# Loads of the opening in another order, one bias row, a later weight conversion and a second buffer for the thresholded low part, in a spectral layer with a gated feed-forward

## The chip, the core and the metric

One NeuronCore of one Trainium2 chip runs the whole program. The time is the device's, in microseconds, for one execution. Engines: TensorE (PE, with its weight loads PEld), VectorE (DVE), ScalarE (ACT), GpSimd (POOL), and SyncE (SP), whose queue issues every DMA of this kernel. Every engine takes its instructions in order.

## What is computed

Eight sequences of 3136 rows of 256 floats go through a spectral layer and a gated feed-forward layer:

```python
X = rfft(x, axis=1)                      # x: 8 x 3136 x 256
Yr = Xr @ w_r - Xi @ w_i + b_r           # w: 256 x 256
Yi = Xr @ w_i + Xi @ w_r + b_i
Y = softshrink(Yr, 0.01) + 1j * softshrink(Yi, 0.01)
x = irfft(Y, n=3136, axis=1)
h = relu(x @ w_in)                       # w_in: 256 x 1024
c = conv3_along_rows(h, conv_w)          # depthwise, 3 taps
out = (h * sigmoid(c)) @ w_out           # w_out: 1024 x 256
```

w_in, conv_w and w_out come as 64-bit floats.

## The kernel before

**Stages.** The transform of 3136 = 56 x 56 points is done in two factors. Stage 1 multiplies x by f1 (seven column groups per batch, `stage1`, for batch 0 `stage1_head`) and stores the result to DRAM (sc1). From there the work runs in 56 steps (batch b, frequency group g of seven): `load_a2` reads a group of sc1 back across the batch (so the first of a batch needs all seven stores of that batch), `stage2` multiplies by t2 and splits the result into a high and a low part (fh, fl), `mix` multiplies by the weights W with three products each, adds the bias and thresholds to v, and splits v into sh (ACT) and sl (GpSimd, line 321), and `stage3` multiplies by inv1 and stores to DRAM (sc2). Then stage 4 and the feed-forward layer (`up`, `down`) run from sc2.

**The loop.** Iteration `it` loads a2 of step it+2, runs stage 2 of step it, mix of step it-1, stage 3 of step it-3 and one or two further groups of stage 1 of a later batch. In its first seven iterations it also loads inv1 of group it (to be split by ACT and DVE, lines 140 and 141) and t2 of group it+1.

**The background.** `later` converts the 64-bit conv_w (cw), w_in and w_out on DVE and ACT, as a generator that is advanced a few pieces in each iteration: 3 x 7 pieces for cw, then nine for each of eight weight tiles, of which one only asks for bits. The bits have two buffers.

**What sets the order.** A planner places the instructions of each engine by the order of the program and by when their inputs are ready in its own forecast, and puts in all waits. `tc.issue_after(ins)` queues what its block traces on the engine of `ins` behind `ins`, on that engine alone: around loads that means SP's queue, around the threshold (line 319) DVE's. SP holds a DMA back until its data may be touched, and all that stands behind it waits too. Buffers: a2 has three, raw (for W and inv1) two, sh two, sl one.

**Lines of the steps below.** 140 and 141 split inv1; 147 loads t2; 153 W; 163 the bias; 168 inv1; 236 x; 245 and 246 stage 1 and its copy by ACT; 265 stores batch 0's stage 1; 270 loads a2; 280 stage 2; 283 to 288 its splitting; 304 mix; 309 adds the bias; 313 combines to v; 319 thresholds; 320 and 321 split v; 331 stage 3.

Of the kernel before, what the change touches and what calls it, by code (L numbers as in the profile page):

```python
# [9 lines left out]
F32 = mybir.dt.float32  # L10
F32R = mybir.dt.float32r
# [3 lines left out]
ALU = mybir.AluOpType  # L15
# [10 lines left out]
UG = 4  # L26
NG = U // UG
# [69 lines left out]
def spectral_ffn_kernel(ctx: ExitStack, tc: tile.TileContext, x, w_r, w_i, b_r, b_i,  # L97
# [19 lines left out]
    with ExitStack() as ab:  # L117
# [14 lines left out]
        cmx.tile([P, 96], F32, name="pad")  # L132
        bias = cmx.tile([P, 2, UG // 2, D], F32, name="bias")
        wmix_hi = cmx.tile([P, NT, 3, D], F32R, name="wmix_hi")
# [11 lines left out]
        def load_t2(g):  # L146
            nc.sync.dma_start(t2[:, g * UG:(g + 1) * UG, :], fwd2v[:, g * UG:(g + 1) * UG, :])
# [12 lines left out]
        def load_bias():  # L160
            for c in range(2):
                for k in range(UG // 2):
                    nc.sync.dma_start(bias[:, c, k, :], (b_r, b_i)[c].partition_broadcast(P))

# [42 lines left out]
        def later():  # L207
# [13 lines left out]
            asked = []  # L221
            for n in range(len(pieces) + 1):
                if n < len(pieces):
                    dst, src, nm = pieces[n]
                    asked.append((dst, load_bits(src, WP, nm), WP, nm))
                    yield None
                if n:
                    yield from split_weight(*asked.pop(0))

# [61 lines left out]
        def mix(xs):  # L291
# [16 lines left out]
            for c in range(2):  # L308
                nc.vector.tensor_tensor(p1[:, c], ps[2], bias[:, c], op=ALU.add)
            for c in range(2):  # L310
# [4 lines left out]
            sh = wk.tile([K2, UG, D], F32R, name="sh")  # L315
            sl = wk.tile([K2, UG, D], F32R, name="sl", bufs=1)
            r = wk.tile([K2, UG, D], F32, name="r", bufs=1)
# [24 lines left out]
        n_it = len(items)  # L342
        WP0, CW_IT = 3, 9
        a2s = {}
        p1 = NG
        load_f1()
        with tc.tile_pool(name="hx", bufs=1, reuse_waits="tile") as hx:
            xh = []
            for p in range(NG):
                xr, ld = load_x(hx, 0, p, parts=2 if p == 0 else 1, tag=f"hx{p}")  # L350
                xh.append(xr)
            with tc.issue_after(ld.ins):
                load_t2(0)
                load_mix()
                load_bias()
                st = stage1_head(xh)
        with tc.issue_after(st.ins):
            for _ in range(2):
                stage1(*items[p1])
                p1 += 1  # L360
            for i in range(2):
                a2s[i], ld = load_a2(*items[i])
        ab.enter_context(tc.issue_after(ld.ins))
# [9 lines left out]
        for it in range(n_it + 3):  # L373
            if it + 2 < n_it:
                a2s[it + 2], _ = load_a2(*items[it + 2])
            if it < n_it:
                xs[it] = stage2(items[it][1], a2s.pop(it))
            if it < NG:
                load_inv1(it)
                if it + 1 < NG:  # L380
                    load_t2(it + 1)
            if 0 <= it - 1 < n_it:
                ss[it - 1] = mix(xs.pop(it - 1))
            if 0 <= it - 3 < n_it:
                stage3(*items[it - 3], ss.pop(it - 3))
            while p1 < n_it and p1 < min(it + AHEAD, NG + 2 + it + it // 2):
                stage1(*items[p1])
                p1 += 1
            if WP0 <= it < n_it:
                with tc.issue_after(ss[it - 1][2].ins):  # L390
                    for _ in range(5 if it < CW_IT else 2 + (it % 5 == 0)):
                        next(background, None)
# [148 lines left out]
```

## Time and profile before

| | us |
|---|---|
| median of three runs | 1771.51 (1766.52 to 1772.43) |
| the profiled execution | 1769.05 |
| its span, first to last instruction | 1767.3 |
| PE busy | 1731.0 (98% of the span) |
| DVE busy | 1524.3 (86%) |
| ACT busy | 1229.1 (70%) |
| GpSimd busy | 134.7 (8%) |

The profile is one execution. Busy time says how long an engine had an instruction under way; the idle time before an instruction is put down to what released it last. Matmuls are pipelined, so PE's busy time counts overlapping instructions once. A DMA's landing is when its data are in place.

### The profile page before, as it was taken

The page shows a single profiled execution, that of the slowest core. Times are in us where ns is not written, and L with a number is a line of the kernel's source. Part 1 is how long each engine was busy: PE and PEld are TensorE (multiplying, and loading weights), DVE is VectorE, ACT ScalarE, POOL GpSimd, SP SyncE. Part 2 cuts the span into 40 slices and gives each one's busy share as a digit, 9 for nine tenths or more (in the row PEclk, how much of TensorE's full clock was granted, in tenths as well). Part 3 has the DMA queues.
Part 4 walks back from the last instruction along what each step waited for, and adds up shares of the span by engine and source line. Part 5 has one row for each costly group of instructions (what it writes and reads, how often), then busy time and mean ns, then how long its engine had stood idle before and what let it go on. Part 6 is the DMA issues. An engine that isn't in the chain of part 4 may idle for free.

```text
span 1767.3 us, 29387 instructions
## 1 busy us (share of the span) xinstructions
PE 1731.0 (98%) x12096; PEld 1621.6 (92%) x12096; DVE 1524.3 (86%) x1820; ACT 1229.1 (70%) x1590; POOL 134.7 (8%) x60
## 2 busy tenths in 40 slices
PE   6899999999998999999999999999999999999999
PEld 2788888888998999999999999999999999999998
DVE  2899999998896988988888888888888888888887
ACT  2667777776665777777777777777777777777766
POOL 0122222222232000000000000000000000000000
PEclk8999999999999999999999999999999999999999
DMA  9777677677534110111111011111101111100001
GB/s 263 216 230 236 196 232 216 192 230 228 164 111 136 43 43 22 32 53 53 32 53 53 22 55 51 49 46 52 43 22 43 53 43 43 42 22 22 22 22 42
DMA packets 107382, 164.63 MB, mean 93 GB/s; under 512 B 8816, under 2 KB 86000, under 8 KB 107248
## 3 DMA queue, kind: packets, MB, share of 16 engines
q1 hardware_dynamic: 107248, 162.74, 30.9%
q8 instruction: 96, 1.57, 0.4%
q14 instruction: 38, 0.31, 0.1%
HBM read 85.65 MB, written 77.07 MB: 92 GB/s over the span
## 4 chain that ended last, share of the span: by engine, by line
PE 93%; DMA 3%; DVE 1%; ACT 1%; issue 0%; SPq 0%; ACTq 0%
PE acc L470 31%; PE ps_h L442 31%; PE ps_mx L304 12%; PE ps_s L423 5%; PE ps_s L280 5%; PE ps_s L331 4%; PE ps_s L245 4%; DMA i_raw<-in_inv_dram 2%; DMA z<-sc 1%; DMA sc<-ha 0%; DMA a<-sc 0%; DMA sc<-a 0%; ACT a L246 0%; DVE cw L212 0%; DVE yl L430 0%
## 5 line engine op out<-in xcount | busy, mean ns | idle before, releaser
L470 PE MATMUL acc<-wout,gh 128*128 128x256 f32 x3136 | 567.0, 280 | 0.0
L451 DVE SCALAR_TENSOR_TENSOR c<-h,cw,c 128x896 f32<-128x896 f32 x448 | 513.1, 1147 | 47.3 <-ACT c L449 46.3
L442 PE MATMUL ps_h<-yh,win 128*128 128x450 f32 x1792 | 551.0, 368 | 0.1
L470 PEld LDWEIGHTS acc<-wout,gh 128*128 128x128 f32 x3136 | 493.7, 188 | 6.5
L470 PE MATMUL acc<-wout,gl 128*128 128x256 f32 x1568 | 437.6, 281 | 0.0
L444 ACT ACTIVATE h<-ps_h 128x900 f32<-128x900 f32 x224 | 207.7, 927 | 254.8 <-PE ps_h L442 254.8
L442 PEld LDWEIGHTS ps_h<-yh,win 128*128 128x128 f32 x1792 | 338.7, 189 | 26.4 <-DVE yl L430 0.8
L442 PE MATMUL ps_h<-yl,win 128*128 128x450 f32 x896 | 329.2, 367 | 0.0
L470 PEld LDWEIGHTS acc<-wout,gl 128*128 128x128 f32 x1568 | 293.7, 188 | 0.1
L457 DVE TENSOR_TENSOR gl<-c,gh 128x896 fp32r<-128x896 f32 x224 | 243.1, 1089 | 53.6 <-ACT gh L456 50.1
L453 DVE TENSOR_TENSOR c<-h,c 128x896 f32<-128x896 f32 x224 | 243.6, 1088 | 46.9 <-ACT c L452 46.7
L456 ACT CAST gh<-c 128x896 fp32r<-128x896 f32 x224 | 209.8, 942 | 49.4 <-DVE c L453 49.4
L452 ACT ACTIVATE c<-c 128x896 f32<-128x896 f32 x224 | 213.3, 952 | 23.9 <-DVE c L451 21.0
L304 PE MATMUL ps_mx<-wmix_lo,fh 128*128 128x256 f32 x672 | 202.2, 301 | 0.0
L304 PE MATMUL ps_mx<-wmix_hi,fh 128*128 128x256 f32 x672 | 196.9, 294 | 0.5 <-DVE v L313 0.3
L304 PE MATMUL ps_mx<-wmix_hi,fl 128*128 128x256 f32 x672 | 188.7, 282 | 1.3 <-DVE fl L288 1.2
L442 PEld LDWEIGHTS ps_h<-yl,win 128*128 128x128 f32 x896 | 168.9, 189 | 11.0
L449 ACT ACTIVATE c<-h,cw 128x896 f32<-128x896 f32 x168 | 175.5, 1044 | 2.6 <-DVE gl L457 0.2
L321 POOL TENSOR_TENSOR sl<-v,sh 128x1024 fp32r<-128x1024 f32 x56 | 134.5, 2402 | 423.1 <-PE ps_s L331 300.0
L313 DVE TENSOR_TENSOR v<-ps_mx,p 64x512 f32<-64x512 f32 x224 | 154.0, 688 | 3.3
L304 PEld LDWEIGHTS ps_mx<-wmix_lo,fh 128*128 128x128 f32 x672 | 126.4, 188 | 12.3 <-issue 12.3
L304 PEld LDWEIGHTS ps_mx<-wmix_hi,fl 128*128 128x128 f32 x672 | 126.0, 188 | 11.8 <-issue 9.9
(84 smaller groups left out, 2023.0 us busy)
## 6 DMA issues: line engine op xcount, KB each, us to landing
a<-sc SPq DMA_DIRECT2D x56, 448.0 KB, 5.0
sc<-z SPq DMA_DIRECT2D x56, 448.0 KB, 3.3
z<-sc SPq DMA_DIRECT2D x56, 448.0 KB, 3.8
xr<-in_x_dram SPq DMA_DIRECT2D x55, 448.0 KB, 4.7
out_dram<-o SPq DMA_DIRECT2D x27, 896.0 KB, 4.0
sc<-a SPq DMA_DIRECT2D x49, 448.0 KB, 4.9
sc<-ha SPq DMA_DIRECT2D x7, 448.0 KB, 7.5
win_bits<-in_moe_w_in_dram SPq DMA_DIRECT2D x4, 512.0 KB, 7.6
```

Source lines behind the costliest of these rows:

```text
L304: nc.tensor.matmul(ps[c][:, k, :], lt, rh, start=(n == 0), stop=(n == len(mm) - 1))
L313: nc.vector.tensor_tensor(v[dst, :, k, :], ps[c][src], p1[src, c], op=ALU.add)
L321: SL_ENG.tensor_tensor(sl, v, sh.bitcast(F32), op=ALU.subtract)
L442: nc.tensor.matmul(ps[:, a, 0:CH + 2], lt, rh, start=(n == 0), stop=(n == len(mm) - 1))
L444: nc.scalar.activation(h, ps[:, :, 0:CH + 2], AF.Relu)
L449: nc.scalar.mul(c, h[:, :, 0:CH], cw[:, 0, f:f + 1])
L451: nc.vector.scalar_tensor_tensor(c, h[:, :, k:k + CH], cw[:, k, f:f + 1], c, op0=ALU.mult, op1=ALU.add)
L452: nc.scalar.activation(c, c, AF.Sigmoid)
L453: nc.vector.tensor_tensor(c, h[:, :, 1:CH + 1], c, op=ALU.mult)
L456: nc.scalar.copy(gh, c)
L457: nc.vector.tensor_tensor(gl, c, gh.bitcast(F32), op=ALU.subtract)
L470: nc.tensor.matmul(acc[m // 2][:, m % 2, :], lt[:, sl], rh[:, f, :], start=(f == 0 and n == 0 and m % 2 == 0), stop=(f == NF - 1 and n == ...
```

## The change

Bias goes from two copies per part to one (two DMAs in place of four), and line 309 reads it with a broadcast over the two halves. In the opening, W is loaded ahead of t2 of group 0; the first a2 load comes right behind batch 0's last store, the bias and the second a2 behind it, and the two stage-1 groups of batch 1 come after them. In the first five iterations t2 of the next group and inv1 of this one are queued on SP behind the a2 load of this iteration, t2 first. The conversion starts in iteration 7 in place of 3, with two and three pieces in turn in place of five (up to iteration 8) and then two or, every fifth time, three. The bits of a weight tile are asked for after five pieces of the one before. sl gets two buffers.

```diff
-        bias = cmx.tile([P, 2, UG // 2, D], F32, name="bias")
+        bias = cmx.tile([P, 2, D], F32, name="bias")
...
             for c in range(2):
-                for k in range(UG // 2):
-                    nc.sync.dma_start(bias[:, c, k, :], (b_r, b_i)[c].partition_broadcast(P))
+                nc.sync.dma_start(bias[:, c, :], (b_r, b_i)[c].partition_broadcast(P))
...
             for n in range(len(pieces) + 1):
+                work = split_weight(*asked.pop(0)) if n else iter(())
+                for _ in range(5):
+                    if n:
+                        yield next(work)
                 if n < len(pieces):
                     dst, src, nm = pieces[n]
                     asked.append((dst, load_bits(src, WP, nm), WP, nm))
                     yield None
-                if n:
-                    yield from split_weight(*asked.pop(0))
+                yield from work
...
-                nc.vector.tensor_tensor(p1[:, c], ps[2], bias[:, c], op=ALU.add)
+                nc.vector.tensor_tensor(p1[:, c], ps[2], bias[:, c].unsqueeze(1).broadcast_to([K2, UG // 2, D]), op=ALU.add)
...
-            sl = wk.tile([K2, UG, D], F32R, name="sl", bufs=1)
+            sl = wk.tile([K2, UG, D], F32R, name="sl", bufs=2)
...
-        WP0, CW_IT = 3, 9
+        WP0 = NG
...
             with tc.issue_after(ld.ins):
+                load_mix()
                 load_t2(0)
-                load_mix()
-                load_bias()
                 st = stage1_head(xh)
         with tc.issue_after(st.ins):
+            a2s[0], ld = load_a2(*items[0])
+        with tc.issue_after(ld.ins):
+            load_bias()
+            a2s[1], ld = load_a2(*items[1])
             for _ in range(2):
                 stage1(*items[p1])
                 p1 += 1
-            for i in range(2):
-                a2s[i], ld = load_a2(*items[i])
         ab.enter_context(tc.issue_after(ld.ins))
...
             if it + 2 < n_it:
-                a2s[it + 2], _ = load_a2(*items[it + 2])
+                a2s[it + 2], ld = load_a2(*items[it + 2])
...
             if it < NG:
-                load_inv1(it)
-                if it + 1 < NG:
-                    load_t2(it + 1)
+                with tc.issue_after(ld.ins) if it + 2 < NG else ExitStack():
+                    if it + 1 < NG:
+                        load_t2(it + 1)
+                    load_inv1(it)
...
                 with tc.issue_after(ss[it - 1][2].ins):
-                    for _ in range(5 if it < CW_IT else 2 + (it % 5 == 0)):
+                    for _ in range(2 + it % 2):
                         next(background, None)
```

## Rows read from the trace of the kernel before

**Rows 1.** The page's first part: busy us (share), instructions.

```profile
PE 1731.0 (98%) x12096; PEld 1621.6 (92%) x12096; DVE 1524.3 (86%) x1820; ACT 1229.1 (70%) x1590; POOL 134.7 (8%) x60
```

**Rows 2.** Busy time by stretch: length, engines busy (instructions), PE clock, DMA share, GB/s.

```profile
23.00:32.60 9.60, 0.00 (x0) 0.01 (x1) 1.18 (x2) 0.34 (x1) 0.00 (x0) 0.71 0.95 317
32.60:42.00 9.40, 7.77 (x25) 5.24 (x26) 1.53 (x3) 2.55 (x6) 0.00 (x0) 0.57 1.10 244
42.00:75.00 33.00, 28.01 (x197) 23.77 (x198) 27.11 (x45) 18.81 (x35) 2.41 (x1) 1.00 0.92 242
75.00:125.00 50.00, 47.51 (x342) 41.09 (x340) 45.74 (x83) 33.91 (x59) 13.75 (x6) 1.00 0.72 210
125.00:390.00 265.00, 265.00 (x1969) 235.76 (x1969) 251.68 (x409) 191.86 (x305) 69.10 (x30) 1.00 0.73 217
390.00:480.00 90.00, 90.00 (x676) 80.59 (x675) 77.79 (x123) 59.93 (x99) 22.88 (x11) 1.00 0.66 195
```

**Rows 3.** PE's waits, whole span: us in total, times, longest.

```profile
PE ps_s L245 <- ACT a L246: 6.0, 5, 2.2
```

**Rows 4.** ACT's waits from 40 to 130 us: total, times, longest.

```profile
ACT i_hi L140 <- DMA i_raw<-in_inv_dram: 12.4, 6, 4.3
```

**Rows 5.** The chain that ended last: start us, us, what.

```profile
24.25 6.40 DMA sc<-ha
...
99.89 3.08 DMA sc<-a
...
102.98 4.20 DMA a<-sc
...
125.69 0.86 PE ps_s L245 x2
126.55 3.39 PE ps_mx L304 x29
```

**Rows 6.** Timeline of PE: start, us, instruction, shape, count [idle before, releaser].

```profile
35.97 3.79 PE L280 MATMUL ps_s<-t,a 112*128 112x128 f32 x16 [1.33 <-DMA a<-sc]
...
41.86 1.13 PE L280 MATMUL ps_s<-t,a 112*128 112x128 f32 x8 [0.28 <-DMA t<-in_fwd_dram]
```

**Rows 7.** Line 163, loads of the bias: durations ns, first and last start, landing.

```profile
L163 SPq DMA_DIRECT2D bias<-in_b_r_dram x2: 346/346/346, 10.1 to 11.7; - x2
L163 SPq DMA_DIRECT2D bias<-in_b_i_dram x2: 328/328/328, 13.4 to 14.8; - x2
...
DMA to landing us min/median/max: 8.0/8.6/9.1
```

**Rows 8.** Line 236 from 24 to 27 us, x of batch 1.

```profile
L236 SPq DMA_DIRECT2D xr<-in_x_dram x2: 893/952/1012, 24.6 to 25.5; - x2
...
DMA to landing us min/median/max: 7.9/8.2/8.4
```

**Rows 9.** Timelines of DVE, ACT and GpSimd within one steady step.

```profile
255.11 1.23 DVE L319 SCALAR_TENSOR_TENSOR v<-v,r 128x1024 f32<-128x1024 f32 x1
...
259.05 0.69 DVE L288 TENSOR_TENSOR fl<-d,fh 128x512 fp32r<-128x512 f32 x1
...
263.19 0.42 DVE L285 TENSOR_TENSOR d<-ps_s,d 128x256 f32<-128x256 f32 x1 [0.74 <-ACT fh L284]
...
264.24 1.23 DVE L319 SCALAR_TENSOR_TENSOR v<-v,r 128x1024 f32<-128x1024 f32 x1
...
256.57 1.06 ACT L320 CAST sh<-v 128x1024 fp32r<-128x1024 f32 x1
...
260.56 2.36 POOL L321 TENSOR_TENSOR sl<-v,sh 128x1024 fp32r<-128x1024 f32 x1 [6.76 <-PE ps_s L331]
```

**Rows 10.** Groups of DVE instructions by line, 400 to 480 us: busy, mean ns, idle.

```profile
L309 DVE TENSOR_TENSOR p<-ps_mx,bias 128x512 f32<-128x512 f32 x18 | 11.5, 682 | 0.0
```

**Rows 11.** GpSimd's timeline at 81 us; durations of line 188 on cw (min/median/max ns).

```profile
81.43 2.36 POOL L321 TENSOR_TENSOR sl<-v,sh 128x1024 fp32r<-128x1024 f32 x1 [3.75 <-PE ps_s L331]
...
L188 DVE SCALAR_TENSOR_TENSOR cw_e<-cw_bits,cw_e x3: 161/167/1744, 82.1 to 110.4; 128x8 int32<-128x8 int32 x3
```

## Prediction, made before the changed kernel ran

> **What bounds the kernel now.** I read the engines' busy times first: TensorE (PE) is busy in 1731.0 of 1767.3 us [rows 1]. So a change that only reorders loads and moves side work can return at most the 36 us in which PE is not busy, and of those only what lies in the part it touches. The stage windows say where they are [rows 2]. From 125 to 390 us, the steady run of loop steps, PE is busy in 265.00 of 265.00 us: nothing is to be had there, only to be lost. The opening holds the rest: PE does nothing from 23.0 to 32.6 us (9.6 us), is busy in 7.77 of 9.40 us up to 42 us at a mean granted clock of 0.57 (partly at the lower of its two levels, after the idle stretch), and then leaves 33.00 - 28.01 = 5.0 us (42 to 75) and 50.00 - 47.51 = 2.5 us (75 to 125). Who ends the later waits: ScalarE's (ACT) copy of the stage-1 result, 6.0 us in 5 waits [rows 3], and ACT itself stands 12.4 us for the loads of inv1, which sit in its in-order queue [rows 4].
>
> **How the opening is chained.** The chain of waits says: the last store of batch 0's stage 1 leaves at 24.25 and lands 6.40 us later, at 30.65 [rows 5]; the first load_a2 reads all seven stores back, and PE's first stage-2 matmul starts at 35.97, released by that load [rows 6]. The loads land one behind the other. The first bias copy lands at 10.1 + 9.1 = 19.2, the last at 14.8 + 8.0 = 22.8 (1.2 us each), the two stage-1 loads of batch 1 at 24.6 + 7.9 = 32.5 and 25.5 + 8.4 = 33.9, and a2(0) at 35.9, 2.0 us after them [rows 6 to 9].
>
> **The change, part by part.**
>
> *Bias loaded once, behind the first a2; stage-1 loads behind it too.* Four bias DMAs ahead of the stores (3.6 us of the DMA queue from the first landing to the last) become two behind a2(0); two 448 KB loads (1.4 us each in the queue) go behind a2(1). With the bias gone the stores could land at 30.65 - 3.6 = 27.0. But the last store's issue at 24.25 also waits for its copy, and a store with an empty queue takes 3.08 us (99.89 to 102.97, same size) [rows 5]: 27.3 is the later of the two. A lone a2 load took 4.20 us (102.98 to 107.18) [rows 5], so a2(0) lands at 27.3 + 4.2 = 31.5 where it was 35.9: **4.4 us earlier**. What is late next is t2(1), which the second step needs. By the new order it stands behind two bias copies (2.4 us at the old rate), a2(1) (2.0), two xr (2.8) and a2(2) (2.0), and takes about 1.0 itself, half of an a2: 31.5 + 10.2 = 41.7, against 41.86 before, when PE's second step started on exactly this load [rows 6]. So the second step does not move; the gain stays only if PE fills 31.5 to 41.7 with work: stage 2 of step 0 (3.79 us at the low clock [rows 6]), mix of step 0 (36 matmuls at 3.39/29 = 0.117 us [rows 5], 4.2 us), two stage-1 groups (8 records at 0.86/2 us [rows 5], 3.4 us): 11.4 us for 10.2. Before, 25 records had run by 42.0 [rows 2]: stage 2 of step 0, four of stage 1 and the first of mix, 6.0 us of it. Upper bound 4.4 us. Lower bound 0: PE's instructions stand in a fixed order, and if stage 2 of step 1 stands ahead of most of mix(0), as it does now (it came after four of the 36), PE waits for t2(1) as before. I take **3.5**, since mix(0) is ready some 2 us sooner than t2(1) lands.
>
> *t2 and inv1 behind the a2 two steps ahead.* The order becomes that of need; at present inv1 of a step and t2 of the next may overtake the a2 that is wanted sooner. Nothing is removed from the queue. What may go is part of ACT's 12.4 us behind inv1 [rows 4] and with it the 6.0 us of PE behind ACT's copies [rows 3]. inv1 itself lands no earlier, so half may well stay. A new wait comes in: a2(3) to a2(6) wait for stage 2 of the step three before to free a buffer, and t2 and inv1 are queued behind them on SP; they are needed a step or more after that (9 us, below), and a load takes 4.2 us alone and 8.4 behind a queue [rows 5, 8], so I cost it at nothing; without that cover such a step would lose up to 4.2 us.
>
> *Conversion from step 7 instead of 3.* It takes cw's chain out of the DVE queue in the stretch from 75 us, where DVE is busy 45.74 of 50.00 us [rows 2], and i2 and the loads of cw out of SP's queue in the opening. Together with the reorder, the 7.5 us that PE leaves between 42 and 125 us are the upper bound, 0 the lower (the waits behind inv1 stay). I take **4**.
>
> *Conversion at 2.5 pieces a step, later bits.* The steady step is 264.24 - 255.11 = 9.13 us [rows 9]. DVE is busy 251.68/265 of it with the conversion (8.67 us) and 77.79/90 after it (7.89) [rows 2]: 0.78 us for 2.2 pieces, 0.355 each. At 2.5 it is 8.78 us, leaving 0.35 us a step. The 93 pieces (3 x 7 + 8 x 9) last 37 steps, to step 43 of 56; stage 4, which takes over that memory and needs the results, comes 12 steps or 110 us later, so the later end costs nothing. Bits asked for five pieces into the previous weight still have over a step to land: nothing, and at worst one wait of about 8 us on DVE at the first weight.
>
> *Bias as a broadcast operand.* 682 ns for 512 elements from PSUM and SBUF [rows 10]; the strided reads of the other lines cost the same per element, so nothing. At worst each of the two halves pays the 0.42 us of a 256-element instruction (line 285) [rows 9], 0.16 more for each of two instructions, 0.3 a step, which would use up the 0.35.
>
> *Two buffers for sl.* Now GpSimd's subtraction waits for stage 3 of the step before: it starts at 260.56 after standing idle 6.76 us for it, though its input was done at 256.57 + 1.06 = 257.63 [rows 9]. With two buffers it starts there and runs 2.36 us, to 260.1. PE gains nothing: stage 3 comes later anyway and PE is full. But DVE has an instruction with two SBUF inputs there, the low part of d (line 288, at 259.05) [rows 9]. The trace shows what such a meeting costs: GpSimd ran from 81.43 to 83.79, and a tiny DVE instruction with two SBUF inputs that started at 82.1 ended with it, after 1.74 us, where the other two of its line took 0.16 [rows 11]. So line 288 would lose about 0.95 us in a step like this; its place moves with the conversion pieces ahead of it (512 elements each, like its own 0.69 us at most), so with three pieces it falls partly or wholly behind the window. Bounds: 0 and 0.95 us a step, against 0.35 us of slack and an idle 0.74 us ahead of line 285 [rows 9]. I take 0.4 on average, nearly all inside the slack: **1 us late** in all, ends 0 and 37 x 0.60 = 22 us.
>
> The Trainium skill (page "SBUF — State Buffer", section "Who interferes with whom") says that a DVE instruction with two SBUF inputs contends with a GpSimd one that reads SBUF, and that the second to issue blocks until the first ends. The 1.74 us row agrees. Taken at its hardest, a meeting in every step, it gives the third rival below.
>
> **Sum.** 3.5 + 4 - 1 = 6.5 us. The profiled execution took 1769.05 us (span 1767.3); the median of the runs is 1771.51, their mean 1770.15. I take the sum from the middle of these: 1770.2 - 6.5, **1764 us**.
>
> **Rivals.** (1) *Given back at the second step.* PE stands at t2(1) with mix(0) behind it, and ACT at inv1(0), which now lands after t2(1), at about 42. The first term is 0 to 1 and the second 0 to 2: 1769. For: the present order has just this form. Against: ACT's 12.4 us were worst where inv1 ran far behind a full queue, and the queue is shorter now. (2) *All of the opening's later waits go.* 4.4 + 7.5: 1758. For: they hang on one engine's order. Against: the DMA share is 0.92 up to 75 us [rows 2], so part is bandwidth. (3) *Slower: DVE becomes the bound.* If GpSimd's new place costs DVE more than 0.35 us in the mean step, PE falls behind by the difference in each of 37 steps. At 0.7 that is 13 us, so 1777; at the full 0.95, 22 us, 1786; with the opening's gain lost as well, more. For: the step shown; against: the piece order shifts line 288 out of the window as DVE falls late. (4) *It does not do what it says*: the planner orders SP's queue as before; 1770.
>
> **How the numbers follow.** Chances: forecast 0.42 (1760 to 1768), rival 1 0.20, rival 2 0.15, rival 3 0.20 (half of it beyond 1776), rival 4 0.03. About 0.3%, 5.3 us, is what a measurement of this kernel can tell from no change: faster means under 1766.2, slower over 1776.8. Faster: three quarters of the forecast's case and all of rival 2, 0.47. Slower: half of rival 3, 0.11. The rest, 0.42, is same. The range 1756 to 1777 leaves out the far half of rival 3 and little of rival 2.
>
> **What would show it.** First stage-2 matmul near 31.5 us (36 before); second near 41; PE's waits for ACT's copies well under 6.0 us; PE idle between 42 and 125 us near 3.5 us. GpSimd's start within 0.2 us of ACT's cast; line 288 at 0.69 us mean if harmless, over 1.2 if not. PE still busy in all of 125 to 390 us. A late DVE there, or a first stage 2 after 34 us, makes the prediction wrong.

## The result: slower, and the profile after

The changed kernel takes 1787.67 us (median; 1786.41 to 1792.21), against 1771.13 for the kernel before: ratio 1.0103, interval 1.0077 to 1.0128. The forecast was 1764 with 1756 to 1777, so it was wrong in sign. The third rival, VectorE as the bound through GpSimd's new place, had named 1786 as its end. Of the experiments below, one execution of e4_opening was slow (1809.56 us) and is left out of its ratio.

The page's engine line and the stretches of [rows 1, 2] (length, engines busy, PE clock, DMA share, GB/s), now of the changed kernel, whose span is 1786.4 us:

```profile
PE 1739.9 (97%) x12096; PEld 1626.2 (91%) x12096; DVE 1545.5 (87%) x1820; ACT 1228.3 (69%) x1590; POOL 135.6 (8%) x60
```

```profile
32.60:42.00 9.40, 6.18 (x23) 5.13 (x23) 2.04 (x4) 1.72 (x4) 0.00 (x0) 0.50 1.00 220
42.00:75.00 33.00, 30.29 (x198) 24.56 (x196) 24.20 (x37) 17.72 (x34) 2.38 (x1) 0.95 1.05 263
75.00:125.00 50.00, 48.19 (x348) 41.64 (x346) 44.07 (x69) 34.66 (x57) 14.29 (x6) 1.00 0.71 209
125.00:390.00 265.00, 258.86 (x1897) 228.32 (x1896) 250.82 (x396) 181.48 (x295) 67.30 (x28) 1.00 0.71 209
390.00:480.00 90.00, 87.85 (x639) 76.89 (x639) 87.23 (x132) 60.60 (x98) 22.67 (x10) 1.00 0.69 206
```

Up to 125 us little has moved. From 125 to 390 us, where PE was busy all the time, it now leaves 6.1 us, and VectorE ends at 87.23 of 90.00 in the next stretch (77.79 before, where the conversion had ended by 395 us; here it runs to 468).

Busy time hides small delays, because a late matmul still overlaps its neighbour. So I also took, for each matmul, the time from its start to the next one's start, less the spacing that its kind keeps in the steady run (0.117 us for mix, 0.112 for stage 2, 0.429 for stage 1), and added it up. This is "PE's lost time" below, worked out from all PE records of each trace, in us (the last column includes the time after 600 us):

| kernel | 0 to 150 | 150 to 500 | 500 to 600 | all |
|---|---|---|---|---|
| before | 31.6 | 0.5 | 11.4 | 47.2 |
| after | 30.9 | 14.9 | 16.5 | 66.4 |

The 19.2 us between them are the difference of the two spans (19.1): the opening gave back 0.7 in place of 7.5, the loop lost 14.4, and the passage into stage 4 another 5.1.

What VectorE did in one step of the loop. GpSimd's line 323 is line 321 of before, 290 is 288, 321 is 319, and 311 is 309 (start, us, instruction; idle time before, and its releaser):

```profile
337.79 1.22 DVE L321 SCALAR_TENSOR_TENSOR v<-v,r 128x1024 f32<-128x1024 f32 x1
339.25 1.28 DVE L311 TENSOR_TENSOR p<-ps_mx,bias 128x512 f32<-128x512 f32 x2
340.45 2.67 DVE L290 TENSOR_TENSOR fl<-d,fh 128x512 fp32r<-128x512 f32 x1
347.40 1.23 DVE L321 SCALAR_TENSOR_TENSOR v<-v,r 128x1024 f32<-128x1024 f32 x1 [0.17 <-ACT r L320]
```

```profile
340.22 2.36 POOL L323 TENSOR_TENSOR sl<-v,sh 128x1024 fp32r<-128x1024 f32 x1 [8.20 <-ACT sh L322]
```

GpSimd runs from 340.22 to 342.58. Line 290 starts 0.23 us after it and ends at 343.12, 0.54 us after GpSimd's end: 2.67 us for work that takes 0.69 [rows 9]. The step, from 337.79 to 347.40, is 9.61 us long; before, a step took 9.13 [rows 9].

VectorE's groups from 200 to 480 us, by form (busy us, mean ns, idle before them), and two rows of the waits over the whole span (us in total, times, longest):

```profile
L290 DVE TENSOR_TENSOR fl<-d,fh 128x512 fp32r<-128x512 f32 x29 | 30.7, 1058 | 0.1
L189 DVE TENSOR_TENSOR wout_m<-wout_m,wout_e 128x512 int32<-128x512 int32 x4 | 4.3, 1067 | 0.0
L185 DVE TENSOR_SCALAR wout_e<-wout_e 128x512 int32<-128x512 int32 x4 | 3.2, 804 | 0.0
L188 DVE TENSOR_SCALAR wout_m<-wout_bits 128x512 int32<-128x512 int32 x4 | 1.7, 422 | 0.0
```

```profile
POOL sl L323 <- ACT sh L322: 430.5, 55, 63.1
PE ps_mx L306 <- DVE fl L290: 7.1, 13, 1.2
```

GpSimd now waits for ScalarE's cast, as the change meant it to (in the whole span it waited once for something else, 7.1 us for PE). PE waits 7.1 us in all for line 290, in 13 waits; in the kernel before it waited once for that instruction, 1.2 us.

### The profile page after: what moved, and what is told of

It reads as the page before. It is cut to its first block, busy times and chain, and to the rows that moved or that the text cites. A ratio compares the mean times of both kernels' runs of the same rounds, so it can differ in the third digit from the quotient of the medians.

```text
span 1786.4 us, 29380 instructions
## 1 busy us (share of the span) xinstructions
PE 1739.9 (97%) x12096; PEld 1626.2 (91%) x12096; DVE 1545.5 (87%) x1820; ACT 1228.3 (69%) x1590; POOL 135.6 (8%) x60
## 4 chain that ended last, share of the span: by engine, by line
PE 80%; DVE 9%; issue 7%; DMA 2%; ACT 2%; SPq 0%; POOL 0%; DVEq 0%; ACTq 0%; POOLq 0%
PE acc L474 31%; PE ps_h L446 31%; PE ps_mx L306 6%; PE ps_s L427 5%; DVE v L315 3%; PE ps_s L333 2%; PE ps_s L247 2%; PE ps_s L282 2%; DVE fl L288 1%; ACT r L320 1%; DVE p L311 1%; DMA wm_raw<-in_w_i_dram 1%; DVE fl L290 1%; DVE d L287 1%; DVE v L321 1%
## 5 line engine op out<-in xcount | busy, mean ns | idle before, releaser
L306 PE MATMUL ps_mx<-wmix_hi,fl 128*128 128x256 f32 x672 | 193.9, 291 | 7.2 <-DVE fl L290 7.1
L306 PEld LDWEIGHTS ps_mx<-wmix_hi,fl 128*128 128x128 f32 x672 | 126.4, 189 | 22.3 <-DVE fl L290 10.8
L282 PEld LDWEIGHTS ps_s<-t,a 112*128 112x128 f32 x896 | 110.1, 194 | 34.8 <-issue 12.6
```

The source lines that it names most:

```text
L282: nc.tensor.matmul(ps[:, k], a2[:, k, t * P:(t + 1) * P], t2[:, g * UG + k, :], start=(k == 0), stop=(k == UG - 1), skip_group_check=True)
L306: nc.tensor.matmul(ps[c][:, k, :], lt, rh, start=(n == 0), stop=(n == len(mm) - 1))
```

## Experiments

The kernel before was timed again with each group of experiments (medians of 1769.22 to 1770.07 us), and the ratios below are to those times. They are taken over all the runs, so they can differ by 0.001 from what two medians give.

**One part at a time.** Four kernels take parts of the change alone or away.

e1_sl_one, the changed kernel with one buffer for sl:

```diff
-            sl = wk.tile([K2, UG, D], F32R, name="sl", bufs=2)
+            sl = wk.tile([K2, UG, D], F32R, name="sl", bufs=1)
```

> The changed kernel with one buffer for sl, as before; all else stays changed. Port theory (GpSimd's subtraction, started right behind ACT's cast, holds up the DVE instructions with two SBUF inputs; 21.6 us lost there in all against 4.5 before): PE is busy again in nearly all of 125 to 480 us, the 18 us of waits between 200 and 520 us go, about 1769 us. Pace theory (2.5 conversion pieces a step make DVE the bound by themselves): nearly all of the loss stays, 1783 to 1788. Order theory (the planner's new order of DVE and PE, whatever GpSimd does): most stays, over 1780.

e2_before_sl_two, the kernel before with the second buffer and nothing else:

```diff
-            sl = wk.tile([K2, UG, D], F32R, name="sl", bufs=1)
+            sl = wk.tile([K2, UG, D], F32R, name="sl", bufs=2)
```

> The kernel before with two buffers for sl and nothing else. Port theory: DVE has 0.46 us of slack a step at the old pace of 2.2 pieces and loses some 0.55 us a step at the new place of GpSimd's work: between 1774 and 1785, PE's waits for DVE appear between 130 and 400 us and end where the conversion ends. Pace theory: 1771, as before. Order theory: 1771 give or take 3.

e3_pace, the changed kernel with the old pace of the conversion:

```diff
-                    for _ in range(2 + it % 2):
+                    for _ in range(2 + (it % 5 == 0)):
```

> The changed kernel with the conversion at 2 pieces a step and 3 in every fifth, still from step 7, two buffers for sl. Port theory: 0.11 us less DVE work in each of 42 steps, so 3 to 6 us come back, 1782 to 1785, and GpSimd still holds up DVE in most steps. Pace theory: the whole loss goes, about 1770.

e4_opening, the kernel before with the new opening and the single bias, and nothing else of the change:

```diff
+            a2s[0], ld = load_a2(*items[0])
+        with tc.issue_after(ld.ins):
+            load_bias()
+            a2s[1], ld = load_a2(*items[1])
...
-                load_inv1(it)
-                if it + 1 < NG:
-                    load_t2(it + 1)
+                with tc.issue_after(ld.ins) if it + 2 < NG else ExitStack():
+                    if it + 1 < NG:
+                        load_t2(it + 1)
+                    load_inv1(it)
```

> The kernel before with the opening of the changed one alone: bias once and behind the first a2, W ahead of t2, stage-1 loads behind the second a2, t2 and inv1 behind the a2 two steps ahead; conversion and sl as before. From the two traces (PE's waits up to 200 us sum to 30.6 us in the changed kernel, 31.8 before) I expect the first stage 2 near 33 us in place of 36 and the gain given back by 55 us: 1770, within 3 of before. If the opening was worth the 7 us that I forecast and something else hid it: 1764.

| kernel | us | ratio to before | lost 0 to 150 | 150 to 500 | 500 to 600 |
|---|---|---|---|---|---|
| e1_sl_one | 1796.15 | 1.0148 (1.0133 to 1.0163) | 30.3 | 23.1 | 16.0 |
| e2_before_sl_two | 1794.56 | 1.0129 (1.0112 to 1.0146) | 33.1 | 16.5 | 18.7 |
| e3_pace | 1798.18 | 1.0152 (1.0136 to 1.0169) | 32.5 | 17.1 | 20.9 |
| e4_opening | 1776.92 | 1.0035 (1.0021 to 1.0050) | 38.4 | 0.6 | 10.2 |

The second buffer alone makes the kernel before as slow as the whole change does, and slower than the 1774 to 1785 us expected. But taking it away from the changed kernel does not mend it, and a slower pace does not either: two misses for the theory in its first form, "the second buffer puts GpSimd into line 290's way". e4_opening is a third miss: it was expected within 3 us of the kernel before and took 6.9 more. It loses 6.8 us more up to 150 us and nothing in the loop. That is not the price of the loads alone, though. About 5 of the 6.8 us fall between 100 and 150 us: from 95 to 150 us GpSimd held five instructions of VectorE for 8.7 us above their undisturbed times (0.8 in the kernel before), PE waited 2.1 us once for VectorE, and its granted clock was 0.83 from 140 to 150 us (1.00 before). The old conversion, five pieces a step there, meets GpSimd too.

Why one buffer doesn't mend it shows in e1's step at 214 us (timelines of GpSimd and VectorE):

```profile
213.77 2.36 POOL L323 TENSOR_TENSOR sl<-v,sh 128x1024 fp32r<-128x1024 f32 x1 [6.78 <-PE ps_s L333]
```

```profile
214.40 2.28 DVE L290 TENSOR_TENSOR fl<-d,fh 128x512 fp32r<-128x512 f32 x1
```

GpSimd does wait for stage 3 of the step before, but VectorE has come late: its threshold started 7.0 us behind the end of mix here, against 5.2 in the undisturbed steps of the kernel before. What made it late is a first meeting one step earlier, with the threshold on time (5.2 us behind mix) and GpSimd at its old place:

```profile
204.64 2.36 POOL L323 TENSOR_TENSOR sl<-v,sh 128x1024 fp32r<-128x1024 f32 x1 [6.77 <-PE ps_s L333]
204.80 2.75 DVE L290 TENSOR_TENSOR fl<-d,fh 128x512 fp32r<-128x512 f32 x1
```

Two pieces of conversion and half of the combination (line 315) stood ahead of line 290 in that step, and so it started 0.16 us behind GpSimd.

From there on the lateness feeds itself. At 214 us stage 3 ends 1.2 us after the cast, where it is 2.9 us otherwise (0.3 us in the next two steps, with the threshold 8.3 us behind mix). GpSimd starts nearly where two buffers would have put it, meets line 290, and keeps VectorE late. The place of GpSimd behind stage 3 is harmless only while the order of VectorE's work keeps line 290 out of it and VectorE is on time. The kernel before met GpSimd there as well (line 288 took 1.28 us at 307.88, with GpSimd at work since 306.24) and is late in single steps, and came back each time in its trace.

e7_one_pace puts both edits, e1's and e3's, into the changed kernel:

> The changed kernel with one buffer for sl and the old pace of two pieces, three in every fifth step, from step 7. With one buffer alone GpSimd still started 0.35 us behind the cast and met DVE, since DVE ran so late that stage 3 had freed the buffer by then. If a late DVE at 2.5 pieces a step was what brought that about: GpSimd is back to about 2.9 us behind the cast, PE is full from 200 to 480 us, and the time is that of the opening alone, 1773 to 1777. If late bits or the later start do it: over 1785.

1795.86 us, ratio 1.0151 (1.0134 to 1.0168). PE lost 0.0 to 0.5 us in each 50 us from 150 to 350 us, and 4.4, 4.2, 6.6 and 8.8 in the four after that. VectorE became late at 330 us, in a step with three pieces of conversion of which one was blocked (line 187, 2.45 us, again with GpSimd at its old place), and stayed late. This is a state that holds itself, and neither the buffers nor the pace alone say when a kernel falls into it. e7_one_pace differs from e4_opening, which lost 0.6 us in the loop, only in the conversion: where it starts, whether it begins with five pieces a step, and when its bits are asked for. With one buffer, then, that decided in these two traces; which of the three, and how, is not shown.

**Is it what GpSimd reads, or only that it runs?** e5_read has GpSimd do one more subtraction behind the cast, into a tile that nobody uses, and e6_write has it read two elements there and then fill that tile twice. Both are the kernel before with one sl buffer; the additions are extra work without use.

```diff
+            junk = wk.tile([K2, UG, D], F32, name="junk", bufs=1)
+            SL_ENG.tensor_tensor(junk, v, sh.bitcast(F32), op=ALU.subtract)
```

> The kernel before, sl with its one buffer, and one more GpSimd subtraction of the same shape and inputs (v - sh) into a spare tile, right behind ACT's cast, ahead of the real one. Its result is not used. So the place of GpSimd's reading is changed and no buffer is. Port theory: as with two buffers for sl (24.5 us slower there): 1785 to 1797, with some 20 us lost by DVE between 200 and 480 us. If it was the second buffer (another layout, another plan): 1770.

```diff
+            tip = SL_ENG.tensor_tensor(junk[:, 0, 0:2], v[:, 0, 0:2], sh[:, 0, 0:2].bitcast(F32), op=ALU.subtract)
+            with tc.issue_after(tip.ins):
+                for _ in range(2):
+                    SL_ENG.memset(junk, 0.0)
```

> As the kernel with the additional subtraction, but GpSimd only touches two elements of v and sh there and then writes the spare tile twice with zeros, so it is busy at the same place, and reads nothing. Port theory with a read port: 1768 to 1773, DVE loses under 2 us between 200 and 480 us. If GpSimd's being busy there (or its writing) was enough: as slow as the one that reads.

e5_read took 1838.8 us (1.0392; 1.0375 to 1.0408), e6_write 1774.68 (1.0031; 1.0016 to 1.0046). Line 288 from 200 to 480 us and GpSimd's timeline, first of e5_read, then of e6_write:

```profile
L288 DVE TENSOR_TENSOR fl<-d,fh 128x512 fp32r<-128x512 f32 x26 | 52.2, 2008 | 0.1
```

```profile
258.03 2.38 POOL L322 TENSOR_TENSOR junk<-v,sh 128x1024 f32<-128x1024 f32 x1 [7.01 <-ACT sh L320]
260.35 2.85 POOL L323 TENSOR_TENSOR sl<-v,sh 128x1024 fp32r<-128x1024 f32 x1
```

```profile
L288 DVE TENSOR_TENSOR fl<-d,fh 128x512 fp32r<-128x512 f32 x31 | 25.7, 829 | 0.1
```

```profile
262.18 0.20 POOL L322 TENSOR_TENSOR junk<-v,sh 128x2 f32<-128x2 f32 x1 [3.14 <-ACT sh L320]
262.44 2.15 POOL L325 MEMSET junk<- 128x1024 f32 x2
264.56 2.38 POOL L326 TENSOR_TENSOR sl<-v,sh 128x1024 fp32r<-128x1024 f32 x1
```

The two fills keep GpSimd busy for about as long as the subtraction would (2.15 against 2.38 us) and at its place, and cost 0.3 per cent. Two subtractions that read cost four per cent. In e6_write line 288 was met once by the second of these fills, and once by a subtraction for sl (a line of VectorE, then one of VectorE and one of GpSimd):

```profile
263.61 0.68 DVE L288 TENSOR_TENSOR fl<-d,fh 128x512 fp32r<-128x512 f32 x1
...
244.64 2.85 DVE L288 TENSOR_TENSOR fl<-d,fh 128x512 fp32r<-128x512 f32 x1
244.44 2.50 POOL L326 TENSOR_TENSOR sl<-v,sh 128x1024 fp32r<-128x1024 f32 x1
```

Its mean of 829 ns comes from that meeting with sl and a short one (865 ns); the other 29 took at most 0.69 us. So it is the reading that does it. e5_read is not a clean price for one meeting, since sl follows at once and makes the blocked window 5 us long.

e8_fl_pool takes the two-input instruction away from VectorE instead: in the changed kernel, line 290 runs on GpSimd.

```diff
-            nc.vector.tensor_tensor(fl[:, :, 2], d, fh[:, :, 2].bitcast(F32), op=ALU.subtract)
+            nc.gpsimd.tensor_tensor(fl[:, :, 2], d, fh[:, :, 2].bitcast(F32), op=ALU.subtract)
```

> The changed kernel with the low part of d (line 290, the DVE instruction that is held up most) on GpSimd, so that DVE has 0.6 us less in a step and meets GpSimd only with conversion pieces. Port theory: PE is full again from 200 to 480 us and the time is 1768 to 1774, unless GpSimd's later delivery of that part makes PE wait for it. If DVE is late for its load or its order alone: 1775 to 1780 from the 0.6 us.

1778.07 us, 1.0042 (1.0027 to 1.0057), 9.6 us under the changed kernel. The theory had said 1768 to 1774; the time lies in the range of its rival, that VectorE is late for its load or its order alone, so by itself this run does not tell the two apart. PE still lost 6.5 us from 150 to 500 us: with more GpSimd work about, conversion instructions are met in line 290's place (line 189 took 1.52 and 1.36 us on average, 0.68 undisturbed).

**GpSimd behind line 288 or 290.** The direct test is to leave the buffers and move only GpSimd's start. The first edit for it misfired, in four kernels. GpSimd first reads two elements of the result of line 288 and then subtracts:

```diff
+                tip = wk.tile([K2, 2], F32, name="tip", bufs=1)
+                q = nxt[1][:, 0, 2, 0, 0:2].bitcast(F32)
+                t0 = SL_ENG.tensor_tensor(tip, q, q, op=ALU.subtract)
+                with tc.issue_after(t0.ins):
+                    SL_ENG.tensor_tensor(sl, v, sh.bitcast(F32), op=ALU.subtract)
```

e12_two_behind is the kernel before with two buffers and this edit, e9_behind_fl the changed kernel with it.

> The kernel before with two buffers for sl (24.5 us slower by itself) and one more edit: GpSimd reads two elements of the low part of d of the next step (line 288's output) before its subtraction, so that it never starts ahead of that DVE instruction. Port theory: the meetings with line 288 are gone, PE is full from 130 to 480 us, 1768 to 1774. If two buffers cost through the plan or the layout: still over 1785.

> The changed kernel with the same edit. Port theory: DVE no longer loses time to line 290 and keeps up at 2.5 pieces a step (8.78 of 9.13 us): the 18 us of waits between 200 and 520 us go, and with them the 5 us more at the passage to stage 4: 1765 to 1770. If 2.5 pieces a step are too many without any meeting: 1775 or more.

1792.98 us (1.0130; 1.0115 to 1.0145) and 1789.05 (1.0110; 1.0095 to 1.0125), as without it. GpSimd's timeline of e12_two_behind says why:

```profile
257.12 2.37 POOL L328 TENSOR_TENSOR sl<-v,sh 128x1024 fp32r<-128x1024 f32 x1 [6.71 <-ACT sh L320]
260.18 0.19 POOL L326 TENSOR_TENSOR tip<-fl 128x2 f32<-128x2 f32 x1 [0.69 <-DVE fl L288]
```

The first of the two lines starts, as ever, right behind the cast. The little read, the second line, ended 6 us ahead of the subtraction that it was to hold back: it reads the low part of the next step, and the one that is met belongs to the step after that. These two decide nothing. e10_old_opening (the changed kernel with the loads in the order of the kernel before, the bits asked for as early as before) and e11_opening (the changed kernel with the split of W behind the head's copies, one stage-1 load ahead of the first a2, and the other moves named below) carry the same edit:

> The kernel before, its opening's loads as before (bias once, at its old place), with the conversion from step 7 at two and three pieces in turn (bits asked for as before), two buffers for sl and GpSimd behind line 288. The later conversion took the PE waits from 100 to 150 us from 7.2 to 1.6 us in the changed opening; here they were 1.8, and 7.7 between 50 and 100: I expect 2 to 6 us off these, 1764 to 1769.

> As the one before it, with another opening: W is split behind the head's last copies (so that DVE never holds PE up by waiting for W, 3.7 us in the changed kernel), one stage-1 load goes ahead of the first a2 while the last stores land, the bias once behind it, then the second a2 and the second stage-1 load. First stage 2 at 31 to 33 us with one stage-1 group done before it: 1759 to 1766. If the second step's t2 sets the pace again: no faster than the one with the old opening.

1792.29 us (1.0131; 1.0114 to 1.0147) and 1793.49 (1.0133; 1.0116 to 1.0150): the loop loses 23.8 and 22.5 us from 150 to 500 and covers all else. Their openings lost 25.9 and 27.8 us up to 150 us, where the changed kernel's lost 30.9.

The corrected edit traces the subtraction one iteration later, behind stage 2, and reads from the step that it meets; the rest stays as above:

```diff
+            if 0 <= it - 2 < n_it:
+                low(ss[it - 2], xs.get(it))
```

e13_two_behind is the kernel before with two buffers and this, e14_behind the changed kernel with this:

> The kernel before with two buffers for sl, and GpSimd's subtraction begun only behind VectorE's low part of d (line 288) of the step that it would meet: GpSimd first reads two elements of that result. The two buffers alone took 1794.6 us and lost VectorE some 21 us in meetings between 200 and 480 us. Theory that the meetings make VectorE late: they fall to under 5 us in that stretch and the time to 1768 to 1776 us. Rival, that a second buffer costs through where tiles lie or in what order VectorE's work is planned: 1785 us or more although the meetings are gone.

> The changed kernel with the same edit: two buffers stay, but GpSimd's subtraction begins behind line 290, the low part of d, of the step that it would meet. Theory that the meetings alone make the changed kernel slow: VectorE's lost time between 200 and 480 us falls from 19 to under 5 us, the time from 1787.7 to 1766 to 1773 us. Rival, that 2.5 pieces of conversion a step are too many for VectorE by themselves, with a conversion that runs until the steps get shorter: 1778 us or more.

| kernel | us | ratio to before | lost 0 to 150 | 150 to 500 | 500 to 600 |
|---|---|---|---|---|---|
| e13_two_behind | 1773.23 | 1.0019 (1.0010 to 1.0029) | 31.9 | 2.4 | 13.0 |
| e14_behind | 1771.52 | 1.0015 (1.0005 to 1.0024) | 31.5 | 1.2 | 14.2 |

By the medians 21.3 us and 16.2 us come back (from e2_before_sl_two and from the changed kernel) with nothing but GpSimd's start moved. The same step of the two kernels, first the changed kernel, then e14_behind (VectorE, then GpSimd):

```profile
159.41 0.90 DVE L290 TENSOR_TENSOR fl<-d,fh 128x512 fp32r<-128x512 f32 x1
164.31 1.23 DVE L321 SCALAR_TENSOR_TENSOR v<-v,r 128x1024 f32<-128x1024 f32 x1 [1.28 <-ACT r L320]
...
157.36 2.39 POOL L323 TENSOR_TENSOR sl<-v,sh 128x1024 fp32r<-128x1024 f32 x1 [7.13 <-ACT sh L322]
```

```profile
159.29 0.68 DVE L290 TENSOR_TENSOR fl<-d,fh 128x512 fp32r<-128x512 f32 x1
163.98 1.23 DVE L321 SCALAR_TENSOR_TENSOR v<-v,r 128x1024 f32<-128x1024 f32 x1 [1.28 <-ACT r L320]
...
160.12 0.20 POOL L333 TENSOR_TENSOR tip<-fl 128x2 f32<-128x2 f32 x1 [6.71 <-PE ps_s L344]
160.27 2.36 POOL L335 TENSOR_TENSOR sl<-v,sh 128x1024 fp32r<-128x1024 f32 x1
```

The threshold before this one starts 0.11 us apart in the two kernels (154.86 and 154.75). A block of 0.22 us on line 290 moves the next one by 0.22 us more, since nothing between took it up: the 1.28 us of idle time ahead of it is the wait for ScalarE's r, which itself waits for v. This holds in steps like this one; where VectorE had put work of the next step into that idle time, more was taken up (a block of 1.28 us at 186.53 moved the next threshold back by 0.26 us only). The changed kernel crept back by about 0.3 us a step from 120 to 200 us, until its threshold started 8.5 us behind mix and the blocks became long. VectorE's groups from 200 to 480 us and the stretches of [rows 2] of e14_behind:

```profile
L290 DVE TENSOR_TENSOR fl<-d,fh 128x512 fp32r<-128x512 f32 x31 | 21.2, 684 | 0.1
L185 DVE TENSOR_SCALAR wout_e<-wout_e 128x512 int32<-128x512 int32 x4 | 1.7, 418 | 0.0
```

```profile
125.00:390.00 265.00, 265.00 (x1976) 236.04 (x1975) 247.92 (x412) 189.43 (x305) 71.02 (x56) 1.00 0.73 218
390.00:480.00 90.00, 90.00 (x678) 80.59 (x677) 86.55 (x141) 64.60 (x103) 25.90 (x22) 1.00 0.69 198
```

PE is busy in all of 125 to 480 us again, with two buffers for sl and 2.5 pieces of conversion a step. A few meetings are left: two instructions in each of the two kernels were held from 200 to 480 us, 3.2 us in all in e14_behind and 3.9 in e13_two_behind. The rival, that 2.5 pieces are too many, falls. That a second buffer costs through where tiles lie or through the planner's order falls as well (e13_two_behind).

**The opening, without the meetings.** e15_old_opening is e14_behind with the loads in the old order (the bias still once) and the bits asked for as early as before; e16_split_late is e15 with the split of W queued behind the last two head copies:

```diff
+                st, cps = stage1_head(xh)
+        with tc.issue_after(cps[0].ins), tc.issue_after(cps[1].ins):
+            split_mix(raws)
```

> As the last, with the kernel before's order of loads and stores in the opening (the bias still once, and a broadcast operand; the conversion from step 7 at two and three pieces, its bits asked for where the kernel before asks). The meetings are gone here too. Theory that the changed opening gained nothing of its own, and that the later conversion is worth the 2 to 4 us of PE's idle time between 42 and 125 us: 1762 to 1768 us. Rival, that 2.5 pieces a step are too many: 1776 us or more.

> The last kernel, with the split of the mixing weight queued behind the last head copies on VectorE and ScalarE, so that no head copy stands behind the wait for that weight. The changed kernel lost 3.7 us of PE at one head copy in that way. Theory that the wait is on the path to the first stage 2: 1 to 3 us under the last kernel, 1760 to 1766 us. Rival, that the stores' landing sets it: the same as the last within 0.3 per cent.

1768.59 us (0.9994; 0.9985 to 1.0003) and 1767.29 (0.9986; 0.9974 to 0.9998). Their loss up to 150 us was 31.0 and 26.5 us. The new order of the loads gained nothing, then: with the old one, and the bits asked for earlier, the median is 2.9 us lower. The medians of e15 and e16 differ by 1.3 us, which is the rival's case, the same within 0.3 per cent; the traced execution of e16 is its fastest (1764.50 us), so the 4.5 us between the two losses say less than they seem to. e16_split_late is the only kernel here whose interval lies wholly under 1; its median is 0.14% under the kernel before. PE's first stage 2 and second step, and VectorE's last head copy and the subtraction of line 160 (157 of the changed kernel), in e16_split_late:

```profile
33.01 3.58 PE L282 MATMUL ps_s<-t,a 112*128 112x128 f32 x16 [1.87 <-DMA a<-sc]
38.87 1.13 PE L282 MATMUL ps_s<-t,a 112*128 112x128 f32 x8 [0.95 <-DMA t<-in_fwd_dram]
...
19.05 0.69 DVE L264 COPY ha<-ps_s1h 112x512 f32<-112x512 f32 x1 [1.02 <-PE ps_s1h L262]
19.66 0.68 DVE L160 TENSOR_TENSOR wm<-wm_raw,wm_raw 128x512 f32<-128x512 f32 x1
```

With the old order of loads the first step starts 3.0 us before [rows 6], and so does the second (41.86 there).

## Why the prediction was wrong

**The term for two buffers (1 us late, ends 0 and 22).** The mechanism was named, its place too; its price was mis-sized, and it was taken for the end of a range instead of the likeliest case. Step by step:

- *What VectorE has to do in a step* was right. The forecast said 8.78 us. In the changed kernel VectorE was busy 272.80 of 280.00 us from 200 to 480 us, where a step took 9.69 us (28 steps from 201.9 to 473.2): 9.44 us a step, of which 0.66 was lost in meetings, so 8.78.
- *What a meeting costs* was put at 0.4 on average, between 0 and 0.95. Measured, as each instruction's time above its undisturbed one: 19.1 us in 280 / 9.69 = 28.9 steps, 0.66 us a step. On line 290 alone it was 29 x (1058 - 684) ns = 10.8 us, or 0.37 a step, which is the forecast's number. The other 8.3 us fell on the conversion's own instructions (lines 185 and 189 above among them), which the forecast left out although [rows 11] had shown just such a one being held. And the top of the range was too low: line 290 took up to 2.67 us, 1.98 lost. (GpSimd's end in the forecast's step, 260.1, is 260.0 by its own terms; nothing hangs on it.)
- *The slack of 0.35 us* was VectorE's idle time by the sum of its work. PE's step without meetings is 9.13 us, so the sum was right, but not all of it can be used: in the late state VectorE still stood idle for 280.00 - 272.80 = 7.2 us, 0.25 a step, the largest part behind ScalarE's r. 8.78 + 0.66 + 0.25 = 9.69; 0.56 more than PE's 9.13, in 28.9 steps 16 us. PE's own count for 150 to 500 us is 14.9.
- *"The piece order shifts line 288 out of the window as DVE falls late"*, which was put against the third rival, is the step of the reasoning that failed most. With GpSimd tied to the cast, which follows VectorE's threshold, the window moves along with VectorE; lateness does not leave it. In the kernel before it is tied to PE's stage 3, and a late VectorE walks into the window. e1 and e7 show that this can happen with one buffer as well, and that the order of the pieces moved VectorE's instructions into a window as well as out of one (line 290 at 204.80 in e1).
- *The passage to stage 4* was not in the sum: 5.1 us more from 500 to 600 us. All kernels in the late state lose 14 to 22 us there (e5, whose steps lie later, aside), the others 9 to 16. The two groups overlap, and why e14_behind still loses 14.2 is open, so these 5.1 us are not shown to come from the meetings.

The Trainium skill (page "SBUF — State Buffer", section "Who interferes with whom") states that of a VectorE instruction with two inputs in SBUF, the on-chip memory, and a GpSimd instruction that reads SBUF the second waits until the first has ended, and that a GpSimd instruction that only writes doesn't count. The 2.67 us and the pair e5 and e6 agree. The prediction had set the rule "at its hardest" against a milder mean; the measurement lies between.

**The opening (3.5 us).** The first stage 2 came at 32.88 where 31.5 was forecast, the second step at 47.18 where 41.7 was. PE's timeline and VectorE's, changed kernel:

```profile
20.01 1.11 PE L262 MATMUL ps_s<-xr,f 112*112 112x512 f32 x2 [3.67 <-DVE ha L264]
32.88 3.78 PE L282 MATMUL ps_s<-t,a 112*128 112x128 f32 x16 [8.78 <-DMA a<-sc]
40.45 2.05 PE L247 MATMUL ps_s<-xr,f 112*112 112x512 f32 x2 [2.93 <-DMA xr<-in_x_dram]
47.18 1.28 PE L282 MATMUL ps_s<-t,a 112*128 112x128 f32 x10
...
18.66 0.69 DVE L157 TENSOR_TENSOR wm<-wm_raw,wm_raw 128x512 f32<-128x512 f32 x1 [5.89 <-DMA wm_raw<-in_w_i_dram]
19.27 0.68 DVE L264 COPY ha<-ps_s 112x512 f32<-112x512 f32 x1
43.68 0.69 DVE L290 TENSOR_TENSOR fl<-d,fh 128x512 fp32r<-128x512 f32 x1 [5.06 <-ACT fh L289]
```

The first time is 1.4 us late: the last store was issued at 24.89, not 24.25, and store and load took 8.0 us, not 7.3. On the way to that store VectorE's subtraction for W stands ahead of a head copy and waits 5.89 us for W, and PE stood 3.67 us behind that copy. The prediction costed W's move at nothing and did not ask what VectorE had queued behind it. In the second step the two stage-1 loads were moved behind the second a2, and nothing was costed for PE's group that waits for them: 2.93 us of PE at 40.45. ScalarE's copy of that group stood ahead of its fh, for which VectorE waited 5.06 us. The gain was given back at the second step, as the first rival said, but not by its mechanism: t2 landed at 45.07, later than the 41.7 of the forecast, and PE did not stand at it. The clock had a part, which the forecast priced for stage 2 alone: it took mix at 0.117 us, from a row of the steady run [rows 5]. PE stood idle for 8.78 and then 2.93 us, and its granted clock was 0.50 from 32.6 to 42.0 us, the lower of its two levels (0.57 before, on average). The stretch up to the second step, first before, then changed:

```profile
42.00:47.18 5.18, 5.01 (x37) 4.31 (x38) 3.49 (x7) 3.83 (x9) 0.00 (x0) 1.00 0.94 169
42.00:47.18 5.18, 5.18 (x25) 3.82 (x24) 1.18 (x2) 2.25 (x4) 0.00 (x0) 0.68 1.10 222
```

PE was busy nearly all of it in both, with 37 matmuls at a clock of 1.00 and 25 at 0.68.

**The later waits (4 us).** PE left 4.5 us between 42 and 125 us, where 3.5 was forecast and 7.5 was left before, so 3.0 of the 4 us came there; but up to 150 us the whole change lost only 0.7 us less. e4_opening, the same opening with the old conversion, lost 7.5 us more than the changed kernel there; since most of that lies between 100 and 150 us, beside the meetings told above, it is no price of either part. ScalarE's wait for inv1 went from 12.4 [rows 4] to 9.4 us in the same stretch, and PE's for ScalarE's copies from 6.0 [rows 3] to 3.7 us, as forecast in direction. But with the old order of loads the later conversion brought 0.6 us by 150 us in one kernel (e15_old_opening) and 5.7 in another with the same opening (e10_old_opening), so the parts don't simply add, and the size of this one stays open. In e15_old_opening PE stood 3.2 us for an a2 load until 108.3 us, and its granted clock was 0.76 from 110 to 115 us; in e10_old_opening that wait was 0.3 us and the clock 1.00 from 95 to 150 us.

**Bias, later bits, pace** cost nothing that shows in the loop. In the loop line 311 took 683 ns where 682 were [rows 10], e14_behind carries all three, and its PE is full from 125 to 480 us.

**Without the meetings** the change is a kernel of 1771.52 us, not 1764: the forecast's 6.5 us would not have come either, but for another reason, the opening.

**The chances.** 0.11 for slower was too low. That the third rival's 1786 lies so near the result is in part luck: it kept the opening's gain and lost 22 us in 37 steps, where the opening gave 0.7, the loop lost 14.4 and the passage to stage 4, which no term had, lost 5.1. The row that decides had been read: a place where a two-input instruction of VectorE lies inside GpSimd's new window, in the one steady step that was looked at.

## What to carry to other kernels

When a change frees an engine to start earlier, look at what it will then run beside, and ask whether the new place follows the engine that it disturbs: if it does, lateness does not cure itself, and the price is paid step after step. Idle time of an engine with a chain through another engine (v, r, threshold) is slack only where other work can be put into it, so compare the loss with what remains without it. A small read of the result that is to be finished first is enough to move a start, if it is the result of the right step; look in the trace for whether the start has moved before reading the time.

## What the runs showed of the hardware

- A subtraction on GpSimd that reads 128 x 1024 elements holds VectorE's two-input instructions of 0.69 us up to 2.67 us in the changed kernel and 2.75 in e1_sl_one. GpSimd is held in turn where it comes second: in e5_read sl took 2.67 us on average from 125 to 390 us, the first of the two subtractions 2.39.
- A VectorE instruction with one input was held too: line 185 (TENSOR_SCALAR, 128 x 512) took 804 ns on average where 418 is its time without meetings. The Trainium skill (page "SBUF — State Buffer", section "Who interferes with whom") lists tensor_scalar among the operations that can take the shared pair of ports; the row agrees.
- Two fills by GpSimd of 0.95 us and more each, at the same place, left line 288 at 0.69 us or less wherever it met them alone, against a mean of 2008 ns with reads.
